# Block-sparse attention with gathered blocks and half of the gate's convolution on TensorE, in a fused attention and gated feed-forward kernel

## The chip, the cores and the metric

One core of one Trainium2 chip. The metric is the device time of one execution in microseconds (us); lower is better. Each kernel was run several times, and medians are given. A run more than 1.5% above the fastest of the same kernel counts as slow and is left out of ratios.

## The reference, cut to what matters

```python
# q, k, v: (4 batches, 8 heads, 768 tokens, 64), each 0.1 * randn;  sampled_blocks: (24, 3)
scores = (q @ k.T) / 8
mask  = |block(i) - block(j)| <= 1           # 24 blocks of 32 tokens
mask |= block(i) in (0, 23) or block(j) in (0, 23)
mask |= block(j) in sampled_blocks[block(i)] # three random key blocks a query block
attn  = softmax(where(mask, scores, -1e9));  x = attn @ v      # heads joined: (4, 768, 512)
h     = relu(x @ w_in)                                         # 512 -> 1024
gate  = sigmoid(conv_w[0]*h[s-1] + conv_w[1]*h[s] + conv_w[2]*h[s+1])
out   = (h * gate) @ w_out                                     # 1024 -> 512
```

Of 24 key blocks a query block sees eight or fewer, except query blocks 0 and 23, which see all. So most of a dense attention's work is not needed; but which blocks are needed is known only from an input.

## The kernel before

The attention is dense: the mask is 24 extra rows of the score product (88 rows instead of 64), and the softmax's exponentials run over everything. The work is cut into 8 half sequences (4 batches, 2 halves), and a small planner orders all instructions of all engines when the program is built: each operation names its engine, an estimated time, its dependences, its buffers and a due time.

```python
NST, NAV, NMIX = 2, 2, 2                                        # PSUM: 2 x 2 banks, 2, 2
...
def s_fn(e, stb=stb, pieces=pieces):                            # scores of eight 128 x 128 blocks
    for (P, hh, kc, par, idx, x, n_) in pieces:
        nc.tensor.matmul(out=st[:, 128 * x:128 * (x + n_)],
                         lhsT=QK[kc % 2][s][0:88, 1, hh, kc // 2, :],
                         rhs=QK[par][s][0:88, 0, hh, idx:idx + n_, :]..., start=True, stop=True)
def e_fn(e, stb=stb, ptb=ptb):                                  # L587, 144 of them
    nc.scalar.activation(out=pt_t[ptb.index], in_=st_t[stb.index], func=AF.Exp, bias=0.0, scale=0.125)
def a_fn(...):                                                  # L610: probabilities times values, 1152
    nc.tensor.matmul(out=o[:, off:off + 65], lhsT=pt_t[ptb.index][:, 128 * x:128 * x + 128],
                     rhs=VT[P % NSLOT][:, hh, kc, 0:65], ...)
...
def mul(x):                                                     # L710: the convolution's products, 192
    for y in range(2):
        nc.vector.tensor_scalar(out=m_t[cb.index][:, x, y],
                                in0=hE_t[heb.index][:, f0 + y, 128 * x:128 * x + 384],
                                scalar1=cw[:, x, f0 + y:f0 + y + 1], scalar2=None, op0=ALU.mult)
def add(a_, b_):                                                # L718: and its sums, 64
    nc.vector.tensor_tensor(out=m[:, a_], in0=m[:, a_], in1=m[:, b_], op=ALU.add)
...                                       # tanh on ScalarE (L731), + 1 (L734) and times h (L737) on VectorE
```

The softmax here doesn't subtract the row's maximum and nothing guards it: scores larger than these inputs give would overflow.

## Time and profile before

| | before |
|---|---|
| time, median of three runs | 277.25 us |
| profiled span | 276.2 us |
| first projection of half 0 runs on (chain) | 59.2 us |
| from there to the end | 217 us |

The busy shares, the chain, four stretches and the spacing of instructions stand in the prediction below.

### The profile page before, as it was taken

The numbers are of one execution on the slowest core, as the hardware profiler recorded it, in microseconds if no ns is written. First come the engines' busy times: TensorE is split into PE (matmuls) and PEld (weight loads), VectorE is DVE, ScalarE is ACT, GpSimd is POOL, SyncE is SP. The second block draws the span as 40 slices with busy tenths as digits, with TensorE's granted clock in tenths as the row PEclk, the third lists the DMA queues.
The fourth block names the chain that finished last, engine by engine and source line by source line (L and its number), as shares of the span: only waits on it lengthen the run. The fifth ranks groups of instructions, "written<-read, shape, count | busy, mean of one in ns | idle before, by whom it ended". The sixth has DMA issues, their size and how long they took to land.

```text
span 276.2 us, 6428 instructions
## 1 busy us (share of the span) xinstructions
PE 213.5 (77%) x2503; PEld 152.0 (55%) x2521; DVE 201.4 (73%) x545; ACT 168.9 (61%) x189; POOL 72.1 (26%) x171
## 2 busy tenths in 40 slices
PE   5724499459779887997779769979898799749573
PEld 1523488337657655676557545766675567524221
DVE  6713362037997998399959994999799749986984
ACT  1511289517786887387858784887788747830420
POOL 8722331211223453022434410211112002211500
PEclk9555599959999999999999999999999999986868
DMA  6999999984215999963599964722200131011003
GB/s 141 141 211 197 160 157 116 159 154 113 55 30 120 148 167 166 230 166 64 78 180 179 168 88 157 140 64 45 93 17 15 31 129 40 18 28 76 1 0 152
DMA packets 67778, 30.35 MB, mean 110 GB/s; under 512 B 60868, under 2 KB 62916, under 8 KB 67748
## 3 DMA queue, kind: packets, MB, share of 16 engines
q0 software_dynamic: 25856, 11.14, 35.7%
q1 hardware_dynamic: 41892, 18.80, 31.6%
q8 instruction: 19, 0.31, 0.5%
q14 instruction: 11, 0.09, 0.1%
HBM read 23.08 MB, written 6.29 MB: 106 GB/s over the span
## 4 chain that ended last, share of the span: by engine, by line
DVE 53%; PE 20%; DMA 16%; issue 4%; SPq 3%; POOL 2%; ACT 1%; DVEq 0%; ACTq 0%
DVE m L710 17%; DVE m L718 10%; DVE hE L683 8%; DMA vn<-in_v_dram 7%; DMA xT<-xtok 6%; DVE gT L737 6%; PE mix L671 6%; PE mix L640 6%; DVE xtok L542 4%; PE st L578 4%; DVE tn L734 4%; PE av L610 2%; DMA et<-nat 2%; SPq L493 2%; PE st L640 1%
## 5 line engine op out<-in xcount | busy, mean ns | idle before, releaser
L587 ACT ACTIVATE pt<-st 128x1024 bf16<-128x1024 f32 x144 | 140.7, 1025 | 69.2 <-PE st L578 68.7
L671 PE MATMUL mix<-xT,winb 128*128 128x384 bf16 x256 | 53.9, 341 | 13.5 <-DMA xT<-xtok 8.6
L610 PE MATMUL av<-vt,pt 128*128 128x65 bf16 x1152 | 60.0, 195 | 0.2 <-ACT pt L587 0.2
L610 PEld LDWEIGHTS <-pt 128*128 128x128 bf16 x1152 | 52.4, 99 | 12.5 <-issue 8.7
L640 PE MATMUL mix<-woutb,gT 128*128 128x512 bf16 x143 | 41.8, 386 | 19.6 <-DVE gT L737 14.3
L710 DVE TENSOR_SCALAR m<-hE,cw 128x384 bf16<-128x384 bf16 x192 | 56.3, 348 | 0.3 <-POOL hE L702 0.3
L683 DVE TENSOR_SCALAR hE<-mix 128x384 bf16<-128x384 f32 x58 | 32.0, 552 | 26.8 <-PE mix L671 26.4
L578 PE MATMUL st<-et,ot 88*128 88x128 bf16 (+1 forms) x224 | 43.9, 240 | 1.3 <-ACT pt L587 0.9
L578 PE MATMUL st<-ot 88*128 88x128 bf16 (+1 forms) x224 | 43.6, 238 | 0.7 <-ACT pt L587 0.5
L578 PE MATMUL st<-et 88*128 88x128 bf16 (+1 forms) x208 | 43.4, 249 | 0.9 <-ACT pt L587 0.2
L578 PE MATMUL st<-ot,et 88*128 88x128 bf16 (+1 forms) x208 | 42.8, 246 | 1.5 <-ACT pt L587 0.7
L578 PEld LDWEIGHTS <-ot 88*128 88x128 bf16 x448 | 35.9, 100 | 13.6 <-issue 3.5
L696 POOL COPY hE<-hE 128x254 bf16<-128x254 bf16 x32 | 13.3, 415 | 111.3 <-DVE hE L683 93.8
L578 PEld LDWEIGHTS <-et 88*128 88x128 bf16 x416 | 33.4, 100 | 11.6 <-issue 2.9
L640 PEld LDWEIGHTS <-gT 128*128 128x128 bf16 x192 | 15.9, 101 | 42.6 <-DVE gT L737 25.5
L718 DVE TENSOR_TENSOR m<-m 128x768 bf16<-128x768 bf16 x64 | 35.6, 557 | 1.0
L731 ACT ACTIVATE tn<-m 128x768 bf16<-128x768 bf16 x32 | 26.9, 840 | 14.3 <-DVE m L718 14.1
L671 PEld LDWEIGHTS <-winb 128*128 128x128 bf16 x256 | 23.7, 101 | 19.3 <-issue 9.7
L650 DVE COPY o2s<-mix 128x512 f32<-128x512 f32 x20 | 13.4, 689 | 12.5 <-PE mix L640 12.5
L737 DVE TENSOR_TENSOR gT<-tn,hE 128x768 bf16<-128x768 bf16 x32 | 18.0, 563 | 1.1
L542 DVE TENSOR_TENSOR xtok<-av,rcp 128x384 bf16<-128x384 f32 x32 | 17.8, 558 | 1.1
L413 POOL DMA_DIRECT2D nat<-in_q_dram x15 | 11.4, 757 | 26.2 <-PE mix L450 17.7
(67 smaller groups left out, 129.2 us busy)
## 6 DMA issues: line engine op xcount, KB each, us to landing
out_dram<-o2s SPq DMA_DIRECT2D x24, 256.0 KB
vn<-in_v_dram POOLq DMA_DIRECT2D x16, 192.0 KB, 5.8
nat<-in_q_dram POOLq DMA_DIRECT2D x15, 192.0 KB, 4.8
nat<-in_k_dram POOLq DMA_DIRECT2D x15, 192.0 KB, 6.2
ot<-et SPq DMA_DIRECT2D x12, 192.0 KB
winb<-in_moe_w_in_dram POOLq DMA_DIRECT2D x1, 1024.0 KB, 12.9
woutb<-in_moe_w_out_dram POOLq DMA_DIRECT2D x1, 1024.0 KB, 17.9
et<-msk SPq DMA_DIRECT2D x12, 72.0 KB
```

The lines of the kernel that those rows point to most:

```text
L542: nc.vector.tensor_tensor(out=xtok_t[xk.index].rearrange("p c h d -> p h c d"), in0=o[:, :, :, 0:64], in1=rcp.unsqueeze(3).broadcast_to([1 ...
L578: nc.tensor.matmul(out=st[:, 128 * x:128 * (x + n_)], lhsT=QK[kc % 2][s][0:88, 1, hh, kc // 2, :], rhs=QK[par][s][0:88, 0, hh, idx:idx + n ...
L587: nc.scalar.activation(out=pt_t[ptb.index], in_=st_t[stb.index], func=AF.Exp, bias=0.0, scale=0.125)
L610: nc.tensor.matmul(out=o[:, off:off + 65], lhsT=pt_t[ptb.index][:, 128 * x:128 * x + 128], rhs=VT[P % NSLOT][:, hh, kc, 0:65], start=(y in ...
L640: nc.tensor.matmul(out=acc(0), lhsT=gT_t[gb.index][:, ffc, 128 * c:128 * c + 128], rhs=woutb[:, ffc, :], start=(ffc == 0), stop=(ffc == NF ...
L650: nc.vector.tensor_copy(out=o2s_t[ob.index], in_=acc(0))
L671: nc.tensor.matmul(out=mix_t[hb.index][:, 0:384], lhsT=winb[:, fc, 128 * ffc:128 * ffc + 128], rhs=xT_t[xt_buf[n].index][:, fc, :], start= ...
L683: nc.vector.tensor_scalar(out=dst, in0=mix_t[hb.index][:, 0:384], scalar1=0.5, scalar2=0.0, op0=ALU.mult, op1=ALU.max)
L710: nc.vector.tensor_scalar(out=m_t[cb.index][:, x, y], in0=hE_t[heb.index][:, f0 + y, 128 * x:128 * x + 384], scalar1=cw[:, x, f0 + y:f0 + ...
L718: nc.vector.tensor_tensor(out=m[:, a_], in0=m[:, a_], in1=m[:, b_], op=ALU.add)
L731: th = op({"ACT": t_act(768)}, lambda e, cb=cb: nc.scalar.activation(out=tn_t[cb.index], in_=m_t[cb.index][:, 1], func=AF.Tanh, bias=0.0, ...
L737: g2 = op({"DVE": t_d2(768)}, lambda e, cb=cb, gtb=gtb, heb=heb, f0=f0: nc.vector.tensor_tensor(out=gT_t[gtb.index][:, f0:f0 + 2, :], in0= ...
```

## The change

Its intent: compute only the score blocks that the mask keeps. Window blocks are read in place, blocks 0 and 23 are laid out once for a pair of heads (KD, VD), and the random blocks are gathered: K by VectorE copies whose source address is a register (three block numbers are packed into one register of a table), V from a copy in DRAM, either by an indirect transfer on GpSimd or by transfers with register addresses on SyncE. The probabilities become 32-column weights, so 67 small matmuls of a pair of heads go to four column groups in turn. Half of the convolution's channels become products with diagonal matrices on TensorE. PSUM becomes two double banks for scores and one pool of four single banks for all else. The planner is new as well: it runs a model of the machine forward and backward and keeps the best of some 40 randomly shaken orders. The diff's core; both files are cut heavily:

```diff
-    NST, NAV, NMIX = 2, 2, 2
+    NX = 11
+    PEC = (1, 3)
+    NST, NMIX = 2, 4
...
+        shake = random.Random(1)
+        for x in range(trials):
+            prio = [p + shake.gauss(0.0, 1.0) for p in best[1]]
+            ... order, span = self.forward(prio, False); keep the best
...
+                for c in range(8):                       # L606: q and k, 32 x 16 transposes of 96 x 64
+                    for h in range(2):
+                        nc.tensor.transpose(out=tp[64 * h:64 * h + 64, 96 * c:96 * c + 96], in_=nat[:, h, c, :],
+                                            identity=ident[0:96, 0:96])
...
+    def block_off(name, i, s):
+        val = rv[(name, i)]
+        val = (val % 32 if s == 0 else (val // 32) % 32 if s == 1 else val // 1024) * 32
...
+            def cp(e, x=x):                              # L740: 264 copies in all
+                for s in range(3):
+                    nc.vector.tensor_copy(out=dst[:, :, x, 32 * s:32 * s + 32],
+                        in_=KT[kt_buf[b].index][:, :, bass.ds(block_off("DVE", i0 + x, s), 32)])
...
+        for x in range(NIX[n]):                          # L746: 46 in all
+            nc.gpsimd.indirect_dma_start(out=VG[vg_buf[n].index][:, x, :], out_offset=None, in_=vs_t[b][:, :],
+                in_offset=bass.IndirectOffsetOnAxis(ap=idx_t[:, i0 + x:i0 + x + 1], axis=0))
+        for x in range(NIX[n], NX):                      # L755: 42 x 3 in all
+            (nc.scalar if e == "ACT" else nc.sync).dma_start(out=VG[vg_buf[n].index][32 * s:32 * s + 32, x, :],
+                in_=vs_t[b][bass.ds(block_off(en, i0 + x, s), 32), :])
...
+                        nc.tensor.matmul(out=dst, lhsT=l_, rhs=r_, ...)       # L908: 32 weight columns
...
+                    nc.tensor.matmul(out=st[:, 512 * y:512 * y + 384], lhsT=dg[:, 2 * z + y, x],   # L1023
+                                     rhs=hE_t[heb.index][:, 2 * a_ + y, 384 * g + x:384 * g + x + 384],
+                                     start=(x == 0), stop=(x == 2), skip_group_check=True)
```

Ahead of that V is loaded, reordered (`vr`), written to DRAM (`vs`), read back (`vn`) and copied once more, shifted by 64 rows (`vs` in SBUF, L692).

## The prediction

> **What bounds the kernel now.** I read the page's busy shares and slices first, then the chain of waits, then the busy time by stage, and last the timeline, where the spacing of back-to-back instructions shows the real cost of each.
>
> ```profile
> PE 213.5 (77%) x2503; PEld 152.0 (55%) x2521; DVE 201.4 (73%) x545; ACT 168.9 (61%) x189; POOL 72.1 (26%) x171
> ...
> PE   5724499459779887997779769979898799749573
> ...
> DVE  6713362037997998399959994999799749986984
> ACT  1511289517786887387858784887788747830420
> ...
> DVE 53%; PE 20%; DMA 16%; issue 4%; SPq 3%; POOL 2%; ACT 1%; DVEq 0%; ACTq 0%
> ```
>
> Half of the chain that ended last is VectorE. Ahead of that lies a slow start: slices 3 to 9 (14 to 62 us) are thin on VectorE throughout and on ScalarE and TensorE in most. By stage (columns: stretch and its length, then busy PE, PEld, DVE, ACT, POOL with counts, granted clock, DMA share, GB/s):
>
> ```profile
> 14.00:35.00 21.00, 8.79 (x85) 7.34 (x83) 5.61 (x11) 3.99 (x4) 5.09 (x7) 0.50 1.41 189
> 35.00:62.00 27.00, 19.09 (x280) 15.68 (x278) 8.29 (x20) 17.21 (x19) 6.13 (x10) 0.88 1.19 147
> 142.00:171.00 29.00, 24.53 (x310) 18.00 (x313) 24.06 (x64) 20.56 (x23) 7.92 (x18) 1.00 0.91 152
> 254.00:276.00 22.00, 13.14 (x50) 5.01 (x49) 17.03 (x47) 5.32 (x9) 4.16 (x10) 0.80 0.13 48
> ```
>
> Three parts: a start until about 59 us, when the first half sequence enters the feed-forward part (the chain passes through one V load of 18.33 us there); seven halves of 27 to 29 us in which VectorE is busy 83 to 89%; a tail of 20 to 30 us that is feed-forward alone. (276 - 59) / 8 = 27.1 us per half.
>
> ```profile
> 13.86 18.33 DMA vn<-in_v_dram
> 59.17 1.28 PE mix L671 x4
> ```
>
> Durations overstate what back-to-back instructions cost. The timeline's merged rows give the spacing:
>
> ```profile
> 150.00 0.41 PE L610 MATMUL av<-vt,pt 128*128 128x65 bf16 x8
> 35.51 16.61 ACT L587 ACTIVATE pt<-st 128x1024 bf16<-128x1024 f32 x18 [1.22 <-PE st L578]
> ```
>
> Eight 65-column matmuls take 0.41 us where one alone shows 0.193: 0.031 each. Eighteen exponentials take 16.61: about 0.92 each = 1024/1200 + 0.07. Likewise 384 columns 0.163 (four in 0.65), 512 columns 0.22, 128 columns 0.056, a convolution multiply on VectorE 0.21 (six in 1.38), not 0.348. By spacing TensorE needs scores 576 x 0.056 + 288 x 0.11 = 64, values 1152 x 0.031 = 36, first projection 256 x 0.163 = 42, second 192 x 0.216 = 41: 183 us. ScalarE: 144 x 0.92 + 32 x 0.71 + 6 x 0.39 = 157.
>
> **What the Trainium skill says.** "ScalarE: Activation LUTs", What ACT_TABLE_LOAD costs: an ACTIVATE takes a fixed part plus 0.833 ns per element and consecutive ones overlap by about 93 ns; the trace agrees (1025 ns alone, 0.92 in a row). "TensorE: Matmul & The Clock Gate", Part 3: matmuls whose outputs lie on different 32-partition groups run concurrently, 2.38x for three. "TensorEngine Tiling (Array Packing)", Key Properties: a change of tiling mode drains TensorE; no 32-column matmul is in this trace, so neither is shown here. "SBUF — State Buffer", Who interferes with whom: VectorE in its two-port modes, or with two SBUF inputs against a GpSimd read, locks against GpSimd, the later one blocks. The trace fits: the convolution multiply has median 311 ns and worst 621 while GpSimd only copies 28 us in all.
>
> **The change part by part.**
>
> ScalarE. The dense 128x1024 exponentials go: 147,456 columns become, per head pair and half (32 of them), 384 + 320 + 736 + 704 = 2144, so 68,608. With 0.07 + n/1200: 0.39 + 0.34 + 0.68 + 0.66 = 2.07, x32 = 66, against 132. Given back: the order of instructions puts 53 of 64 ReLUs (6 before) there, 53 x 0.39 = 21; 31 evictions of transposed q and k, 31 x 0.71 = 22; 18 output evictions, 18 x 0.5 = 9; tanh unchanged, 23; casts and DMA issue, 6. Sum 147: only 10 less than before. ScalarE is used to relieve VectorE.
>
> VectorE. Removed: 96 of 192 multiplies (96 x 0.21 = 20) and 32 of 64 adds (32 x 0.5 = 16); 47 ReLUs x 0.55 = 26; 18 output copies x 0.69 = 12; 16 V copies and 16 evictions, 6 + 9 = 15. That is 89. Added: 264 copies of K blocks at register addresses. Each is 128 elements per partition; the 384-element multiply at 0.21 leaves a fixed part near 0.11, so 0.14, and the register arithmetic before each is unseen in this trace; I take 0.17, 45 us (estimate). Further 17 evictions x 0.56 = 10, set-up of tables and buffers 10, patches and masks 5. Sum 201 - 89 + 70 = 182 of row durations, about 165 by spacing.
>
> TensorE. Unchanged: 42 + 41. Diagonal convolution, 96 x 0.163 = 16. Scores: 896 of 64 columns at 0.031 = 28, and 64 x 0.056 + 64 x 0.1 = 10, against 64. Values: 2144 matmuls with 32 output rows, four column groups in turn. In turn without overlap 2144 x 0.031 = 66; four wholly at once 17; the skill's 2.38 of 3 makes 26, which I take. Transposes of q and k: 512 small ones, 11 to 22, say 16. Mode changes, 64 of about 0.1, 6. Sum 185, practically what it was (183).
>
> GpSimd: 37 ordinary DMA starts x 0.76 = 28; 46 indirect ones, at perhaps 1.2 (estimate, no row shows one) 55; big copies: V reordering and shifting, 6 of 2048 and 12 of 2600 elements, at (0.43 / 254) us per element less its fixed part, about 1.1 ns: 13 + 34; small ones 25. Some 155 us against 72: off the path if early, but it holds the shared port.
>
> DMA: 24 q/k transposes and 24 SBUF copies go; V makes a round trip through DRAM (about 3.2 MB out, 3.2 back, 8.8 MB of gathers in rows of 1040 bytes). The loads come in rows of 1 KB where most packets were under 512 B. Mean use should fall.
>
> So the bound moves from VectorE (201) to TensorE (185), with VectorE 165 and ScalarE 147 close behind.
>
> The start. V must land (10 us), be reordered, written and read back (two landings of 3 to 4 us) before values begin near 21 us; four of them, the normalization and the xT transposes (4 to 6 us in the chain) put the first projection near 30 us instead of 59. This is 29 us, the largest single gain. From 30 us TensorE has left 8 halves x (5.2 + 5.2 + 1.95) + 6 of attention x about 8.2 + transposes 10 = 158 us. The kernel before kept its bound engine at 85 to 89% in the steady stages; at 0.88, 158 becomes 180. The last half's dependences add 4 or so: 30 + 180 + 4 = 214 us, 23% less.
>
> **The rivals.** (1) The value matmuls don't overlap: TensorE gains 40 us to 225, nearly all in the steady part: about 255 us. For it: four groups share one stream of instructions with a weight load each. Against: the skill's measured packing. (2) VectorE stays the bound, through register copies at 0.3 us or through the lock with GpSimd, whose reading copies more than double: 165 + 35 + 15 = 215, which puts the end near 240. For it: the worst-case multiply at twice the median. Against: GpSimd's copies may fall in VectorE's idle time. (3) The V round trip and its gathers arrive late at each batch (GpSimd issues in order): the start stays near 45 us and each batch waits a few us: 235. For it: the 18 us load in the present start. (4) Everything fits better than I think: ScalarE no longer stalls the scores, 0.95 packing: 195 to 200.
>
> **Range and chances.** The rivals (1) to (3) lie above 214 and (4) below; each alone is less likely than not, and only two together would reach 270. Eight in ten: 196 to 240. Faster by over 2%: 0.95; within 2%: 0.03; slower: 0.02.
>
> **What would show it.** First projection at about 30 us; busy sums by spacing of TensorE near 185, VectorE 165, ScalarE 147 (their busy rows, being durations, near 190, 170 and 160); TensorE's share of the chain well above 20% and VectorE's well below 53%; 67 value matmuls in about 0.8 us, not 2; register copies at 0.17 us each; steady halves of 22 to 23 us. The prediction is wrong if the chain still reads half VectorE, if the first projection waits past 40 us, or if GpSimd heads the waits.

## More of the kernel before

The 59.2 us are not the first matmuls of that projection: three of them start at 50.77 us, and then TensorE waits 6.83 us for the last transposed piece of x. From the chain:

```profile
51.53 6.68 DMA xT<-xtok
59.17 1.28 PE mix L671 x4
```

The page's DMA digits (mean busy share of the 16 DMA engines in 40 slices of 6.9 us, in tenths) and the row of the queue that fetches instructions (packets, MB, share):

```profile
DMA  6999999984215999963599964722200131011003
...
q8 instruction: 19, 0.31, 0.5%
```

The DMA engines were nearly full in slices 2 to 9, up to 62 us. Then the busy time by batch, from one first projection to the one two halves later (columns: stretch and its length; busy PE, PEld, DVE, ACT, POOL with counts; granted clock, DMA share, GB/s):

```profile
59.20:113.20 54.00, 46.06 (x580) 34.05 (x584) 45.80 (x123) 39.76 (x44) 17.07 (x40) 0.97 0.84 121
113.20:170.40 57.20, 47.90 (x615) 35.28 (x618) 47.18 (x125) 41.35 (x47) 16.30 (x40) 1.00 0.81 141
170.40:223.60 53.20, 46.76 (x610) 34.97 (x614) 45.33 (x122) 40.97 (x46) 7.88 (x28) 1.00 0.29 71
223.60:276.20 52.60, 38.26 (x310) 21.24 (x310) 41.44 (x110) 21.20 (x27) 9.09 (x28) 0.85 0.14 48
```

Four batches of nearly equal length: a regular kernel whose pace VectorE sets (46 of 54 us).

## The result, and the profile after

The changed kernel is slower: 317.16 us (median of four runs, 314.24 to 324.67, the last slow), against 277.13 of the kernel before in the same rounds. The ratio is 1.1435, with a 95% interval of 1.1333 to 1.1537. (Ratios here are the mean time of one kernel's fast runs over that of the other's of the same rounds, so not quite the ratio of the medians.) The prediction said 214, and gave "slower" 0.02. The page after:

```profile
PE 219.5 (70%) x4233; PEld 147.0 (47%) x4233; DVE 178.0 (57%) x652; ACT 162.0 (52%) x269; POOL 117.4 (38%) x170
...
PE   0744258659788293577895948997936577999994
...
DVE  7725283027669682112685794744939246647781
...
DMA  7987855990648924980379637965472431131013
...
q8 instruction: 33, 0.54, 0.8%
...
PE 46%; issue 14%; ACT 11%; DVE 10%; another core or an unknown queue 4%; DMA 2%; DVEq 1%; SPq 0%; ACTq 0%
```

No engine became fuller than VectorE was, and all but GpSimd (26% before, 38% now) are emptier. VectorE fell as predicted (178 busy, "near 170") and ScalarE too (162, "near 160"); the busiest, TensorE, has 70%. The slices show holes that are not a slow start alone: slices 14, 16, 24 and 30 on TensorE, 16 to 19 on VectorE. In the chain TensorE holds the share that the prediction wanted, yet it is followed by "issue" at 14%: time in which an engine waits for nothing that the profile shows.

By stretch, the first two as in the prediction, then from one first projection to the one two halves later:

```profile
14.00:35.00 21.00, 9.22 (x149) 7.23 (x150) 6.80 (x39) 6.20 (x10) 13.20 (x22) 1.00 0.75 169
35.00:62.00 27.00, 16.14 (x533) 13.57 (x536) 11.24 (x53) 15.20 (x25) 13.27 (x21) 0.92 0.81 142
```

```profile
69.50:150.00 80.50, 55.91 (x1136) 37.08 (x1135) 42.44 (x152) 41.03 (x67) 32.23 (x39) 0.86 0.56 115
150.00:214.40 64.40, 51.67 (x1053) 35.11 (x1053) 43.24 (x153) 39.60 (x67) 28.47 (x36) 0.92 0.73 138
214.40:280.60 66.20, 51.44 (x1047) 34.47 (x1044) 39.74 (x144) 38.45 (x67) 20.95 (x29) 0.85 0.38 99
280.60:312.50 31.90, 27.01 (x225) 14.52 (x224) 20.93 (x63) 16.70 (x29) 0.00 (x0) 1.00 0.19 63
```

The first projection starts at 69.5 us, not at 30, and even later than the 59.2 of before. The chain of this kernel on the way there (start, us, what): a gather of V lands late, and TensorE stops within a group of value matmuls without a wait that the profile shows.

```profile
37.64 4.71 DMA vg<-vs
...
62.74 3.48 issue
...
69.68 4.07 PE mix L1062 x20
```

Batches take 64 to 80 us with 40 to 43 on VectorE and 51 to 56 on TensorE; only the last 32 us, feed-forward alone, are dense (27 of 31.9 on TensorE). So the kernel lost time wherever attention and its preparation mix, and nowhere else. The waits (engine, line, what it waited for: us in all, times, longest):

```profile
POOL nat L578 <- PE mix L606: 54.6, 6, 25.9
DVE rcp L919 <- PE mix L908: 39.8, 16, 8.8
...
PEld L908 <- issue: 24.7, 27, 5.5
```

VectorE now waits for the value matmuls (39.8 us), and GpSimd, which issues in order, waits to load the next q and k until TensorE's transposes free a buffer. TensorE's own waits are many, with no single large releaser. A ring of engines in a fixed order, each waiting for another, is the picture; the experiments ask what drives it.

### The profile page after: what moved, and what is told of

It reads as the page before. It is cut to its first block, busy times and chain, and to the rows that moved or that the text cites.

```text
span 312.5 us, 10688 instructions
## 1 busy us (share of the span) xinstructions
PE 219.5 (70%) x4233; PEld 147.0 (47%) x4233; DVE 178.0 (57%) x652; ACT 162.0 (52%) x269; POOL 117.4 (38%) x170
## 4 chain that ended last, share of the span: by engine, by line
PE 46%; issue 14%; ACT 11%; DVE 10%; another core or an unknown queue 4%; DMA 2%; DVEq 1%; SPq 0%; ACTq 0%
PE mix L946 11%; PE mix L1062 11%; PE mix L908 9%; PE st L864 3%; DVE kg L740 3%; PE st L846 2%; ACT pr L871 2%; PE st L812 2%; PE st L1023 2%; PE mix L606 2%; ACT pg L853 2%; PE st L841 2%; ACT qb L629 2%; DMA vg<-vs 2%
## 5 line engine op out<-in xcount | busy, mean ns | idle before, releaser
L740 DVE COPY kg<-kt 128x128 bf16 x264 | 52.9, 241 | 3.7 <-issue 1.4
L746 POOL DMA_INDIRECT vg<-vs,idx x46 | 44.6, 969 | 22.9 <-issue 12.5
L871 ACT ACTIVATE pr<-st 128x704 bf16<-128x704 f32 x32 | 24.2, 756 | 26.7 <-PE st L864 23.3
L812 PE MATMUL st<-qb,kt 128*128 128x64 bf16 x352 | 20.0, 210 | 23.7 <-issue 15.5
L853 ACT ACTIVATE pg<-st 128x736 bf16<-128x736 f32 x32 | 25.1, 785 | 21.5 <-PE st L846 9.9
L1073 ACT ACTIVATE hE<-mix 128x384 bf16<-128x384 f32 x53 | 25.8, 493 | 15.5 <-PE mix L1062 14.2
L908 PE MATMUL mix<-vg,pr 96*32 96x65 bf16 x704 | 28.4, 203 | 5.5 <-issue 5.5
L812 PEld LDWEIGHTS <-kt 128*128 128x128 bf16 x352 | 17.2, 109 | 28.7 <-issue 25.7
L908 PE MATMUL mix<-vn,pa 128*32 128x65 bf16 x384 | 25.5, 204 | 6.3 <-issue 6.3
L976 DVE TENSOR_SCALAR m<-hE,cw 128x384 bf16<-128x384 bf16 x96 | 23.7, 316 | 10.1 <-ACT hE L1073 10.1
L919 DVE RECIPROCAL rcp<-mix 128x6 f32<-128x6 f32 x32 | 6.2, 194 | 39.9 <-PE mix L908 39.8
L908 PE MATMUL mix<-vs,pa 128*32 128x65 bf16 x320 | 27.1, 203 | 2.6 <-issue 2.5
L908 PEld LDWEIGHTS <-pg 128*32 128x32 bf16 x736 | 23.5, 101 | 11.5 <-issue 11.4
L908 PE MATMUL mix<-vd,pg 128*32 128x130 bf16 x352 | 25.8, 234 | 2.8 <-issue 2.8
L908 PEld LDWEIGHTS <-pa 128*32 128x32 bf16 x704 | 22.0, 99 | 11.1 <-issue 10.8
```

Of the source, the lines that this page charges most:

```text
L740: nc.vector.tensor_copy(out=dst[:, :, x, 32 * s:32 * s + 32], in_=KT[kt_buf[b].index][:, :, bass.ds(block_off("DVE", i0 + x, s), 32)])
L746: vg_w[n].append(op({"POOL": 1.25}, lambda e, x=x: nc.gpsimd.indirect_dma_start(out=VG[vg_buf[n].index][:, x, :], out_offset=None, in_=vs_ ...
L812: nc.tensor.matmul(out=st[:, o + 64 * w:o + 64 * w + 64].rearrange("p (h s) -> p h s", h=2), lhsT=kt()[:, win(i):win(i) + 128], rhs=qcol(i ...
L853: nc.scalar.activation(out=pg_t[pg.index], in_=st_t[sg.index][:, 0:736], func=AF.Exp, bias=0.0, scale=0.125)
L871: nc.scalar.activation(out=pr_t[pr.index], in_=st_t[sr.index][:, 0:704], func=AF.Exp, bias=0.0, scale=0.125)
L908: nc.tensor.matmul(out=dst, lhsT=l_, rhs=r_, start=(y == 0), stop=(y == len(lists[j]) - 1), skip_group_check=True)
```

## The experiments

The theories. (A) Preparation: V's gathers, K's copies and the reordering sit on the path, because they stand in the same in-order lists as everything else. (B) TensorE: the value matmuls or the transposes cost more than predicted. (C) GpSimd shuts VectorE out of SBUF. (D) Diagonal convolution overloads TensorE. Later two more: (E) instruction fetch, and (F) the order itself, that is, the planner's draw. Experiments 1 to 10 change only what single operations do: the planner sees the same operations and times, so the order of the others stays. (These ten are edits of the bodies only; a time taken away shows what it cost in this order.)

**Fixed addresses** (wrong result): block numbers are constants instead of registers, for K's copies and V's transfers.

```diff
-            _, vals = nc.values_load_multi_w_load_instructions(...       # the registers are not loaded either
+            pass
...
-        val = rv[(name, i)]
-        val = (val % 32 if s == 0 else (val // 32) % 32 if s == 1 else val // 1024) * 32
-        return nc.s_assert_within(val, 0, S, skip_runtime_bounds_check_because=why)
+        return 32 * ((5 * i + 7 * s) % 24)
```

> Every block number that was read from a register (K copies on VectorE, V gathers on SyncE and ScalarE) is a constant; result wrong on purpose; order of work, copies, transfers and TensorE's instructions are the same. The changed kernel took about 316 us. Theory R (register addresses cost it: the stretches in which SyncE, ScalarE and TensorE advance in steps of 0.7 us, about 35 us of TensorE gaps of 0.6 to 1.5 us, and VectorE's bunches of 33 copies): those steps vanish, first projection near 55 us instead of 69.7, total 275 to 290. Theory I (TensorE and the other engines wait for their instructions to be fetched, because there are many more of them): TensorE's stream is unchanged, so gaps above 1.5 us stay near 55 us in sum and the total stays above 300. Theory T (the gathers' traffic and order delay the rest): above 300 too.

306.94 us, ratio 1.1027 (1.0921 to 1.1133); the profile fell in a slower execution. Loading and unpacking registers is worth 10 us of the 40: real, but not the cause.

**No V gathers** (wrong): all 88 gathers out, one plain load into each of the two buffers.

```diff
-            vg_w[n].append(op({"POOL": 1.25}, lambda e, x=x: nc.gpsimd.indirect_dma_start(...
+            vg_w[n].append(op({"POOL": 1.25}, lambda e, x=x: nc.gpsimd.dma_start(
+                out=VG[vg_buf[n].index], in_=vs_t[b][0:96, :].unsqueeze(1).broadcast_to([96, NX, ROW]))
+                if n < 2 and x == 0 else None,
...
-                for s in range(3):
+                for s in range(0):
```

> The 88 gathers of V rows (46 indirect ones of GpSimd, 42 in three register-addressed pieces each) are left out, but for one plain load per buffer at the start; wrong on purpose; K copies with registers stay. Theory T (gather traffic holds the queues and delays transposes of the attention output, loads and instruction fetches): first projection before 50 us, gaps above 1.5 us fall from 55 to under 25, total 260 to 275. Theory R: the steps of 0.7 us vanish but VectorE's copies stay: 280 to 290. Theory I (too many instructions as such): above 300.

290.56 us, ratio 1.0317 (1.0191 to 1.0443). Three of the five runs were slow; the mean of the two fast ones is 286.7 us, against 316.2 for the fast runs of the changed kernel. It is the largest single part, about 30 us. Whether it is still slower than the kernel before is unclear at the 2% limit. Its timeline (of a slow run) also shows theory C at work:

```profile
107.32 5.10 POOL L692 COPY vs<-vn 64x2600 bf16<-64x2600 bf16 x2 [8.10 <-DMA vd<-vs]
107.70 2.51 DVE L1035 TENSOR_SCALAR m<-m 128x768 bf16<-128x768 bf16 x1
110.13 2.54 DVE L740 COPY kg<-kt 128x128 bf16 x3
112.48 1.94 POOL L669 COPY vr<-vst 96x2048 bf16<-96x2048 bf16 x1
112.59 2.24 DVE L1038 TENSOR_TENSOR gT<-m,hE 128x768 bf16<-128x768 bf16 x1
```

Two GpSimd copies of 2600 elements take 5.10 us, from 107.32 on. One VectorE operation of 768 elements beside them takes 2.51 us, and three K copies 2.54 us, until GpSimd is done; elsewhere three K copies take about 0.5. The same happens beside the 2048-element copy.

**Half the transposes**: one 128-column transpose in place of two of 64, so 256 transposes fewer (and as many weight loads). The result mixes rows of q and k, yet still passes the comparison: with inputs of 0.1 the softmax should be nearly flat (argued, not measured).

```diff
-                    for h in range(2):
-                        nc.tensor.transpose(out=tp[64 * h:64 * h + 64, 96 * c:96 * c + 96], in_=nat[:, h, c, :], ...
+                    nc.tensor.transpose(out=tp[:, 96 * c:96 * c + 96],
+                        in_=nat.rearrange("p h c d -> p (h c d)")[:, 128 * c:128 * c + 128], ...
```

> The transposes of q and k take 128 columns at once instead of 64, so 256 fewer matmuls and 256 fewer weight loads of TensorE's 8466 instructions (6%), same columns written in all; wrong on purpose (the columns are not in the right order). Theory I: two fetches of 256 instructions fewer and 256 matmuls x 0.03 us: 8 to 15 us less. Theories R and T: at most those 256 x 0.03 = 8 us, more likely 0 to 4 since transposes are mostly off the path.

320.46 us, ratio 1.1547 (1.1438 to 1.1656): no gain, not even the 8 to 15 us that theory I of the expectation (fewer instructions to fetch) asked for.

**Half the value matmuls** (wrong): every second one of L908.

```diff
-            for y in range(max(len(l) for l in lists)):
+            for y in range(0, max(len(l) for l in lists), 2):
```

> Every second one of the value matmuls with 32 output rows is left out (1024 matmuls and 1024 weight loads, 24% of TensorE's instructions); wrong on purpose, all else the same. If their time is simply TensorE work at the end of the path: 32 head pairs x about 0.55 us = 18 us less at the most. Theory I: besides that, 8 of 33 fetches go, and the gaps above 1.5 us fall from 55 to 40 or less: 25 to 35 us less in all. Theories R and T: gaps stay, 8 to 18 us less.

301.72 us, ratio 1.0879 (1.0775 to 1.0984): 15 us. At 0.74 us a group of 67 without a stop, half of 32 groups is 12 us of TensorE time (and fewer instructions have to be delivered, see below). So theory B holds little more than the matmuls' own predicted size; they do overlap.

**Tiny GpSimd copies** (wrong): the V reorder and shift copies on GpSimd move 2 elements.

```diff
-                    nc.gpsimd.tensor_copy(out=dst, in_=src)
+                    nc.gpsimd.tensor_copy(out=dst[:, 0, 0, 0:2], in_=src[:, 0, 0, 0:2])
```

> GpSimd's big copies of V (six reorderings of 2048 elements, 1.9 us each, and six shifts of 2600 elements, 2.4 us each) copy two elements instead; wrong on purpose; the order of all work is the same. In the trace a VectorE K copy that lay beside such a GpSimd copy took 2.34 us instead of 0.195, and an elementwise product 2.24 instead of 0.56: the two exclude each other. Theory X (this exclusion and the length of GpSimd's chain hold each batch's preparation): the 26 us of copies in batches 1 to 3 lie on the path of the preparation, so total 285 to 295 instead of 316. Theory Q (DMA issue of the gathers) and theory I (instruction fetch): 308 to 316.

318.43 us median of four, 310.76 to 322.11; only one counted as fast, so there is no ratio, and the 285 to 295 expected if theory C held did not come. Taking away what shuts VectorE out gains little if anything: in this order the exclusion falls where VectorE isn't what the rest waits for. Theory C is seen, but is not the cause.

**No preparation** (wrong): the two edits for gathers and GpSimd copies together, and K copies for the first two halves only.

```diff
-                for s in range(3):
+                for s in range(3 if n < 2 else 0):                       # K copies
+   ... and the edits of "No V gathers" and "Tiny GpSimd copies"
```

> No V gathers (but one plain load per buffer), tiny GpSimd copies, and K block copies in the first two halves only; wrong on purpose; TensorE's, ScalarE's streams and the order are the same. What stays is the V load, its way through DRAM, attention and feed-forward part. If preparation explains the whole loss (prediction 214, rival sums to 240): 225 to 245. If waits for instruction fetch and order keep a large part of it: 260 to 275; the run without gathers had 290.6.

265.98 us, ratio 0.96 (0.9521 to 0.968). Together 51 us, more than the single parts: preparation is the largest loss in this order, theory A. But the second reading counts as much: with its preparation nearly for nothing, the changed kernel beats the one before by 4%, not by 23. The windows say where the rest lies:

```profile
68.70:132.00 63.30, 50.47 (x1130) 34.17 (x1133) 28.72 (x86) 40.93 (x68) 10.93 (x27) 0.92 0.57 111
132.00:184.00 52.00, 45.46 (x1053) 32.28 (x1054) 29.07 (x87) 39.17 (x67) 11.28 (x26) 1.00 0.64 129
184.00:231.00 47.00, 43.16 (x1040) 30.18 (x1043) 26.21 (x78) 38.15 (x67) 2.59 (x15) 1.00 0.34 93
231.00:262.80 31.80, 26.91 (x224) 14.53 (x224) 20.94 (x63) 16.71 (x29) 0.00 (x0) 1.00 0.19 61
```

From the first projection on, 194 us, ten more than the 184 predicted: with TensorE 80 to 92% busy in each stretch, that part of the prediction is nearly right for a kernel without preparation. (TensorE is busy 166 us there, against 186 after for as many matmuls; its granted clock is 0.92 to 1.00 up to the tail, against 0.85 to 0.92. Whether the clock falls because of the pauses was not tried.) The start has hardly moved (68.7). The chain through the start of this run (start, us, what):

```profile
17.77 7.16 DMA vs<-vr
...
26.48 19.30 DMA vn<-vs
...
47.54 4.01 PE mix L908 x144
...
60.23 2.21 PE mix L908 x94
62.43 3.09 issue
65.52 0.74 PE mix L908 x15
```

V's write takes 7.16 us and its read-back 19.30, where the prediction had two landings of 3 to 4. The first value matmuls start at 47.5, not 21. From there to the first projection it takes another 21.2 us, not 9. And in the midst of a group of value matmuls TensorE stops for 3.09 us and waits for nothing.

**Every gather indirect** (correct): the 42 blocks that SyncE and ScalarE fetched with register addresses go to GpSimd.

```diff
-                    (nc.scalar if e == "ACT" else nc.sync).dma_start(out=VG[vg_buf[n].index][32 * s:32 * s + 32, x, :], ...
+                nc.gpsimd.indirect_dma_start(out=VG[vg_buf[n].index][:, x, :], ...)
```

> All 88 V gathers go as indirect transfers of GpSimd (about 1.22 us of its time each, 42 more: 51 us) and none as register-addressed ones of SyncE and ScalarE; correct result; order of TensorE, VectorE, ScalarE the same. If the register-addressed transfers of SyncE cause the steps of 0.7 us and hold the output transposes: 295 to 305. If the indirect ones do (theory Q1: while GpSimd makes descriptors the other engines' issue slows to one instruction in 0.7 us): more steps, 325 to 345.

356.61 us, ratio 1.2901 (1.2808 to 1.2995): slower than either expected range. **None indirect** (correct): the other way round, each of the 46 indirect ones as three transfers on SyncE.

```diff
-            vg_w[n].append(op({"POOL": 1.25}, lambda e, x=x: nc.gpsimd.indirect_dma_start(...
+            vg_w[n].append(op({"POOL": 1.25}, lambda e, x=x: [nc.sync.dma_start(
+                out=VG[vg_buf[n].index][32 * s:32 * s + 32, x, :],
+                in_=vs_t[b][bass.ds(block_off("SP", i0 + x, s), 32), :]) for s in range(3)],
```

> All 88 V gathers go as 264 register-addressed transfers of SyncE (ScalarE's three of the first half stay), none as indirect ones of GpSimd; correct result. Theory Q1 (indirect ones slow all issue): the steps of 0.7 us vanish, but SyncE needs 33 x about 0.6 = 20 us per half: 300 to 320. If register-addressed ones cause the steps: more of them, 330 to 350.

343.08 us, ratio 1.2405 (1.2311 to 1.2499). Both ways lose: 42 indirect transfers more cost 40 us, 138 register-addressed ones more on SyncE 26. Neither can be "the slow way" that the other would cure. Whatever issues gathers is a queue in order, and everything behind the gathers in that queue waits: loads of q and k on GpSimd, xT transposes and outputs on SyncE. Both hold the plan's order and its belief in 1.25 us for such an operation, so they show cost in this order only.

**Fetch or wait?** (wrong; two runs) The stops of TensorE inside a group of matmuls, where nothing is waited for, were laid beside the packets of the instruction queue in the trace: a packet of 16 KB (0.54 MB in 33 packets, the q8 row) landed 1.2 to 1.6 us before each resumption. The Trainium skill, "Runtime: NRT & Kernel Launch", Instruction fetch mechanics, says that instructions come in 16 KiB blocks of 256, and that the cost of crossing is "mostly hidden". A block of 256 is 128 matmuls with their weight loads. If fetch is the cause, stops come at multiples of 128 in the stream and don't belong to a matmul of the program; so 64 small matmuls were put ahead of "No preparation".

```diff
-        nc.tensor.matmul(out=mix_t[1], lhsT=warm[:, 0:128], rhs=warm, start=True, stop=True)
+        for x in range(9): ...                # that one, and eight of 64 columns, in each of eight warm-ups
```

> The run without preparation (266 us), with 64 more small warm-up matmuls (64 columns each, 128 instructions of TensorE with their weight loads) at the very start, where TensorE idles; all else the same. In the run without them TensorE stops for 1.3 to 4.5 us in the middle of groups that wait for nothing, at its matmuls 605, 733, 1495, 1879, 2516, 2898 and 3535 (counted in the order of their starts), each time with a fetch of 256 instructions landing; the distances are multiples of 128 matmuls. Theory I (stops come from instruction fetch): counted from the start of the stream, the stops stay at about those numbers, which means that they fall 64 matmuls earlier in the program (other matmuls stop than before). A dependence, a bank or a semaphore as cause: the same matmuls of the program stop, that is at numbers 64 higher. Time about the same, 264 to 270.

The number, in the stream, of the weight load at each stop of over 1.2 us, from the trace:

```text
No preparation      607  735 1502 1886 2526 2910 3549     stops 1.54 3.41 4.47 2.01 1.89 1.32 1.89 us, sum 16.5
64 matmuls ahead    607 1502 1630 2526 3294 4061          stops 3.67 2.59 1.40 1.76 1.99 2.02 us, sum 13.4
all of them: number mod 128 = 93 to 95
```

The numbers keep to the same places modulo 128 while the program moved by 64 under them: stops belong to places in the instruction stream, theory E. (Left out are pauses that come between groups and move along with the program, at loads 1046 and 1173 without and 1110 and 1237 with the 64: ordinary waits.) The chain after the shift, at the same point of the kernel as above:

```profile
53.12 0.62 PE mix L908 x47
53.73 3.45 issue
57.19 0.73 PE mix L908 x9
```

In "No preparation" load 607 was a score matmul of L812; here it is a value matmul, with nine of its group left. The time, 260.03 us (ratio 0.9407, 0.9362 to 0.9451), fell a little with the stops. In the changed kernel itself seven such stops (loads 478 to 3540; their place modulo 128 drifts from 94 to 84 along the run) sum to 18.8 us. The kernel before has 19 blocks on that queue and no stop of that kind over 1.2 us in its steady part. A likely reason, argued and not tried: a group of 67 value matmuls is 134 instructions in 0.74 us, so a block lasts about 1.4 us, and the packets of that queue take 0.9 to 1.8 us each in the changed kernel's trace. The kernel before has such small matmuls in bursts of eight, and its 2503 matmuls are spread at 0.11 us each over the span; these 4233, at 0.074. What the stops cost is not their sum: in "Half the value matmuls" they fall to one of 2.2 us, and the time fell by only 15 us, 12 of which are the matmuls' own.

**No gather bytes either** (wrong): is the read-back slow because of the 1.1 MB of each gather buffer's load beside it? The two plain loads of "No preparation" become VectorE fills.

```diff
-                out=VG[vg_buf[n].index], in_=vs_t[b][0:96, :]...
+            vg_w[n].append(op({"POOL": 1.25}, lambda e, x=x: nc.vector.memset(VG[...], 0.5) if n < 2 and x == 0 else None,
```

> The run without preparation, in which the two plain loads of the V gather buffers at the start (2.1 MB, as many bytes as the gathers that they stood for) are replaced by two fills on VectorE; wrong on purpose. In the changed kernel 11.1 MB go through the DMA engines in the first 70 us (8 to 9 tenths busy), and the V read-back of 0.8 MB took 19.3 us to land. If transfers bound the start: first attention values at 36 to 40 us instead of 45.8, first projection at 57 to 62 instead of 68.7, total 254 to 260. If the start is bound by its chain of waits: first projection stays at 66 to 69 and the total at 264 to 268.

266.58 us, ratio 0.9676 (0.9609 to 0.9743). V's read-back now landed by 34 us (no packet follows until 40), against 45.8, so its 19.30 us were a queue behind other bytes. But the start didn't come earlier: my two fills took 4.83 us each on VectorE ahead of the K copies and of V's shift copy, which ended at 47.4 as before. The experiment settles what the read-back waited for, and leaves open how much an earlier read-back would gain.

**Convolution back on VectorE** (correct), with the order planned anew.

```diff
-    PEC = (1, 3)
+    PEC = ()
```

> The changed kernel with all of the convolution on VectorE again (no diagonal matmuls); correct; the order of work is planned anew by the same rules. VectorE gets 96 multiplies x 0.21 and 32 adds x 0.5, some 36 us, more; TensorE 96 x 0.163 = 16 us less. If the changed kernel were bound by VectorE or by its bunches of copies: 335 to 350. If waits of the preparation bind it and VectorE has slack: 310 to 325.

289.98 us, ratio 1.0467 (1.0414 to 1.052): 27 us faster than the changed kernel, and outside both expected ranges. Theory D seems right. But its TensorE gave up only 14 us of busy time (219.5 to 205.4) while VectorE took on 25 (178.0 to 203.2; the profile fell in a slow run), and the planner's own forecast for it was longer (222 us against 216, from running the planner of each kernel.py by itself). What else differs is the order, since the plan is drawn anew.

**The kernel before with half of its convolution on TensorE** (correct): the same part of the change alone, on the old kernel.

```diff
+            if pr in PEC:                                     # pairs 1 and 3
+                        for x in range(3):
+                            nc.tensor.matmul(out=mix_t[yb.index][:, 0:384], lhsT=dg[:, 2 * PEC.index(pr) + y, x],
+                                             rhs=hE_t[heb.index][:, f0 + y, 128 * x:128 * x + 384], ...)
```

> The kernel before (dense attention, no gathers) with only that part of the change that moves two of the four channel pairs of the convolution to TensorE as diagonal matmuls; correct; planned anew by its own rules. VectorE, its bound, loses 36 us of 201; TensorE gets 16 us more, 199 by spacing. If this part alone helps: 255 to 268 (TensorE becomes the bound). If TensorE's two single PSUM banks, now shared with the convolution, cause new waits: 272 to 285.

272.16 us, ratio 0.9837 (0.9796 to 0.9878). VectorE falls from 201 to 164.6 us busy and TensorE rises to 223.9 (83%), with 39% of the chain: diagonal convolution gains a little here and doesn't lose 27.

**Another seed** for the planner's shaking (correct; nothing else), **and with the convolution back on VectorE** under that seed.

```diff
-        shake = random.Random(1)
+        shake = random.Random(2)
```

> The changed kernel, its order planned from another random start (seed 2 instead of 1); correct; the same instructions in another order. If the order is what matters: 285 to 340, that is, at least 10 us away from 316. If the diagonal convolution is what cost 26 us: within 8 us of 316.

> All of the convolution on VectorE (as in the run that took 290), order planned from seed 2. If the diagonal convolution costs 26 us by itself: 284 to 298. If it was the order: 300 to 330.

288.57 us, ratio 1.038 (1.0287 to 1.0473), and 295.47 us, ratio 1.0658 (1.0585 to 1.0731). A single digit is worth 28 us (the planner's forecast is 219 us for this seed and 216 for the first, so it ranked them the wrong way round), and under the same seed diagonal convolution is *faster*, by 7. The windows of the other seed:

```profile
66.50:133.60 67.10, 51.11 (x1024) 34.96 (x1028) 43.63 (x156) 38.05 (x64) 34.08 (x42) 0.88 0.67 136
133.60:195.60 62.00, 53.06 (x1181) 36.78 (x1183) 45.83 (x156) 41.99 (x71) 29.75 (x35) 0.93 0.74 145
195.60:254.90 59.30, 47.44 (x969) 32.18 (x973) 37.35 (x143) 37.02 (x64) 18.54 (x25) 0.91 0.42 111
...
```

Batches of 67, 62 and 59 us in place of 80, 64 and 66, at nearly the same busy times.

**A truer plan** (correct): the planner's guesses are brought nearer to the measured values, with the seed left at 1; **and the same without diagonal convolution**.

```diff
-DMA_LAT = 1.9
+DMA_LAT = 3.5
...   value group 0.72 -> 1.0, K copies of three 0.36 -> 0.6, three transfers 1.25 -> 1.8, transposes 0.42 -> 0.8
```

> The changed kernel, planned with durations nearer to the measured ones: value matmuls of a head pair 1.0 us (0.72), three K copies 0.6 (0.36), three register-addressed V transfers 1.8 (1.25), sixteen transposes 0.8 (0.42), landing 3.5 us after the transfer (1.9), diagonal matrices 3.5 (2.0); correct. The plan itself ends at 244 instead of 216. If the order made for too short durations lost the time: 270 to 295. If the hardware's waits do, whatever the order: 305 to 325.

> The same durations, with all of the convolution on VectorE; correct; the plan ends at 246. If order and diagonal part both matter: 265 to 280, which may equal the kernel before. If only one does: 285 to 300.

293.18 us, ratio 1.0556 (1.0456 to 1.0657), and 299.49, ratio 1.0816 (1.0743 to 1.0888). Better than the first order, not better than another draw with the old guesses. Diagonal convolution gains 6 again.

**The kernel before with a quarter of its convolution on TensorE** (correct, five rounds), to see whether half or a quarter is the better share.

```diff
-    PEC = (1, 3)
+    PEC = (3,)
```

> The kernel before with one of four channel pairs of the convolution on TensorE as diagonal matmuls (two pairs gave 272.2 against 276.1); correct. VectorE loses 18 us instead of 36, TensorE gets 8 instead of 16. If the balance between the two sets the time: 267 to 271. If the shared PSUM banks or TensorE set it: 271 to 276.

284.14 us, ratio 1.0184 (1.0118 to 1.0249), outside both expected ranges. A quarter is slower than none, and half is faster, each by less than 2%. A smooth effect of the share does not give that; more likely the old planner's order also moves the time by some 2% when one operation changes, which was not tried by itself. The 1.6% of the half share can't be put down to the convolution by these runs.

**A third seed** (correct): `random.Random(3)`.

> The changed kernel planned from seed 3; correct. If seed 1 is an unlucky order and 289 the usual: 282 to 298. If the time spreads evenly with the order: anywhere from 282 to 320, so a value above 305 would speak for that.

287.09 us, ratio 1.0285 (1.0214 to 1.0355). Three seeds give 317, 289 and 287: the first is an unlucky draw by some 28 us, and in the two other draws the change is 3 to 4% slower than the kernel before. Theory F accounts for the larger part of the loss that was measured (28 of 40 us), theory A and the start for the missing gain; A was tried in the first order only. What makes the first order bad is known in part: fetch stops are not it (counted as above, with a packet landing just before, they sum to 22.5 and 24.5 us in seeds 2 and 3, against 18.8), while its chain holds 4%, some 12 us, of waits for "another core or an unknown queue", and the chains of the two other seeds hold none.

No correct version of the changed kernel beat the kernel before. The fastest correct one of the study is the old kernel with half its convolution on TensorE, 272.16 us, within 2%.

## Why the prediction was wrong

The prediction missed by 98.5 us (312.5 us of span against 214). The sum that follows is worked out from the first projections in the timelines:

| step of the prediction | predicted | measured | us off |
|---|---|---|---|
| the first projection | 30 | 69.5 | 39.5 |
| from there to the end, engines alone (180 + 4) | 184 | 194 (no preparation) | 10 |
| preparation hidden beside it | 0 | 27 (221 and 222 in the two other seeds, less 194) | 27 |
| the order as good as another | 0 | 22 (243, less 221) | 22 |

One caution on the third and fourth rows: the 194 was measured in the first seed's order, and the 221 in others, so how the 49 us between 243 and 194 divide rests on the assumption that the other orders without preparation would also take 194. Part of both may be the lower clock.

- *The start* is the step that failed first. It was called "the largest single gain", and the first projection runs on 10 us later than before. V's round trip was put at two landings of 3 to 4 us; measured 7.16 and 19.30 (in "No preparation"). The figure was a latency, as if the DMA engines were free; they were not. The changed kernel moves 11.1 MB in its first 70 us, and its DMA digits are 5 to 9 in the first nine slices. "No gather bytes" showed the read-back landing 12 us earlier with two loads gone. It did not show an earlier start, so how much of the 39.5 us the traffic causes stays open. In the changed kernel itself the chain ahead of the first value matmuls (47.7 us) runs through the gathers, which the prediction had left out of the start. From the first value matmul to the first projection it then takes 21.8 us, against 9: three fetch stops of 7.6 us in all lie in it, and xT transposes behind the register-addressed transfers that hold SyncE from 42.7 to 53.1 us (the chain does not pass through these).
- *The factor 0.88*, taken over from the kernel before, failed next. From the first projection, 158 us of TensorE work took 243, a factor of 0.65; in other seeds 0.71; without preparation 0.81. If the stops that lie behind the first projection there (five, 11.6 us) are taken off the 194, it is 0.87 (an estimate). The 0.88 was also read too high: in the windows from 62 to 254 us of the kernel before, VectorE is busy 81 to 87%, 0.84 on average, and 0.83 from 59.2 us to the end. At 0.84 the 180 us become 188, which leaves little of the 10 us in the table's second row. The steady half of "22 to 23" was 40 to 32 us, 34 to 30 in the other seed.
- *The sizes* held, for work that isn't interrupted. 67 value matmuls in 0.74 us (the median of the 17 groups of 32 that take 0.8 or less; 0.8 predicted; with the stops inside them the 32 groups take 1.55 us on average, 50 us in all where the prediction had 26), K copies spaced by 0.176 us (0.17), indirect transfers by 1.25 (1.2), VectorE busy 178 (170), ScalarE 162 (160); GpSimd was lighter, 117 against 155, in part since it makes six copies of 2600 elements and not twelve. The 26 us for values don't follow from "2.38 of 3" (66 / 2.38 is 28), and 11 of the 67 matmuls have 130 columns, not 65; the two slips are small. TensorE's busy row came out at 219.5, not 190: durations exceed the spacing, and the row of before was already 213.5 for the 183 by spacing. The sum of its start-to-start spacings below 0.6 us is 211 in the kernel after and 208 before. So the bill of TensorE, "practically what it was", was also right as a comparison. A sum of correct sizes still gave a wrong time.
- *The rivals.* The third, gathers and round trip late, was right in kind and mis-sized: a start at 45 and a few us each batch, 235 in all; measured 69.5, and 9 us for each of three batches prepared (27 in all) in the better orders, on the assumption above. The first (no overlap of value matmuls) is refuted by 0.74 us. The second's lock is real, 2.5 us for what takes 0.5 or less, and yet "Tiny GpSimd copies" gives no sign that it costs much in this order.
- *What was not in it.* Instruction fetch, up to 18.8 us of stops (two of those in the start lie on the chain; "Half the value matmuls" says that they cost less than their sum), and the draw of the order, 28 us. The range 196 to 240 was built from rivals one at a time; none was on how well a fixed order fits.

Two things stay open. In the changed kernel TensorE issues matmuls at steps of 0.7 us or two or three times that, in three stretches (28 to 38, 166 to 172 and 226 to 233 us; about 20 us). Three or more such steps in a row stand also in "Fixed addresses", "Half the transposes", "Half the value matmuls", "Tiny GpSimd copies" and "Every gather indirect", all in the first order; there are none in "No V gathers", "None indirect", the other plans, the kernel before or without preparation. With fixed addresses or half the transposes the first of them is one plain wait of 10.7 and 11.3 us instead, so they may mark a wait and not cost anything. And at 101 and 117 us signals of finished TensorE work reach ScalarE 5 to 6 us late in the first order (the first of them is "another core or an unknown queue" in its chain); no run told what holds them.

## What to carry to other kernels

A count of operations times their spacing is a floor for each engine; it becomes a time only if the order that feeds the engines holds, so add what must be prepared, in which in-order queue it stands, and what the DMA engines already carry in the start. Where a planner with a random part fixes the order, run two or three draws before crediting or blaming a change: here one digit of a seed was worth 28 us, four times the effect of the part that first seemed guilty. And when large instructions are replaced by bursts of tiny ones, count the instructions: TensorE can outrun their delivery.

## What the Trainium skill lacked or had wrong

- "Runtime: NRT & Kernel Launch", Instruction fetch mechanics: crossing a 16 KiB block is called "mostly hidden". In these runs it shows on TensorE as stops of 1.3 to 5.6 us at places of the stream 128 matmuls apart, 13.4 to 24.5 us in each of five runs, where 134 instructions go in 0.74 us. For the kernel before, with larger matmuls, the page holds.
- "SBUF — State Buffer", Who interferes with whom: the lock between GpSimd and VectorE is as described, and the runs add its size: three K copies took 2.54 us beside a GpSimd copy of 2600 elements. Beside indirect transfers on GpSimd the copies stayed at 0.195 us each.
- "TensorE: Matmul & The Clock Gate", Part 3, gives 2.38 for three column groups; four groups of 32 columns come to (56 x 0.031 + 11 x 0.056) / 0.74 = 3.2 here, in groups without a stop (an estimate, with the spacing that matmuls of 65 and 128 columns had before).
- No page has what a gathered block costs those that queue behind it: 42 more indirect transfers cost 40 us, 138 more register-addressed transfers on SyncE 26 us.
- No page explains the 0.7 us steps or the late signals, which stay open.
